# x @ w_in of later items as three float32r products of exactly split factors, with the first sums scaled in PSUM

## Chip, core and metric

The kernel runs on one core of one Trainium2 chip. The metric is device time in microseconds for one launch, inputs and outputs in HBM. The kernel before has a median of 511.81 us over three runs (511.08 to 513.34).

## What is computed

An mLSTM cell is followed by a two-layer block. B = 4, H = 8 heads, S = 768 steps, D = 40; the 3072 tokens have 320 features, w_in is 320 x 2048, w_out 2048 x 320. Everything is float32, w_in and w_out arrive as float64 bits.

```python
for t in range(S):                       # the cell, per batch and head
    m_new = maximum(f[t] + m, i[t])
    f_stab, i_stab = exp(f[t] + m - m_new), exp(i[t] - m_new)
    C = f_stab * C + i_stab * outer(v[t], k[t])
    n = f_stab * n + i_stab * k[t]
    y[t] = sigmoid(o[t]) * (C @ q[t]) / maximum(abs(n @ q[t]), 1)
x = y as (B * S, H * D)                  # 3072 x 320
h = x @ w_in
out = (h - tanh(h)) @ w_out
```

## The kernel before, in words

The cell is worked in 24 units, each 128 tokens of one batch; two units make a token group g (256 tokens, 12 groups). The features of x lie on partitions: `xT[g % 6]` is 128 x 3 x 256, three overlapping blocks of features. The 2048 hidden features are eight pairs p of two 128-wide blocks (i = 0, 1). One step of the block is a group with a pair, (g, p), 96 in all. An **item** is two such steps done together (the first two items have one), 49 items, numbered x = 0 to 48. From item 17 on an item is (g, p) and (g, p + 1) of one group, four items per group: pairs 0 and 1, 2 and 3, 4 and 5, 6 and 7, for g = 4 to 11.

For an item, `up` (line 1084) makes h: per pair and block two full products of 128 features (line 1099, with the weight column chosen by `col`, the x block by `at`) and a rest of 64 features (line 1099 or, in quarters, line 1104). `ph[i]` is a PSUM bank of 128 x 512: two pairs of 256 tokens. There is one such bank per block, so the next item may start on a bank only when it has been read. `shrink` (line 1160) makes g = h - tanh(h): ScalarE squares (`z`, then `q`), VectorE makes `gt` from h and z (the cube) and then from q. `sums_of_g` adds four more VectorE sums (`s`). `down_seven` (line 972) multiplies with w_out by a seven-product scheme, k = 0 to 6, 14 products per item; products 3 to 6 use the sums `s`, products 0, 1 and 2 use gt alone. It runs one item later (LAG = 1): while item x is in `up`, item x - 1 becomes ready for `down_seven`. At the last item of a group, `put_together` reads the result banks on ScalarE and VectorE and stores.

Items 0 to 16 and units 0 to 11 are ordered by a planner (class Plan, line 157): each operation has an engine, an assumed duration, what it comes after and a rank; the planner simulates the engines and takes the operation that can start first, ties by rank, lower first. From item 17 the order is written out in the loop at line 1576: TensorE's steps of one iteration (`dense`) are the item's `up`, its rests with the scores of a new unit (`crossed_scores`), the rest of the unit scored before (`block_turned`), and `down_seven` of item x - 1. Steps of other engines are spread over iterations with `spread_over` at positions x0 to x1 counted in items, and `merge` (line 1207) sets them between TensorE's steps by the share of the assumed cost that is done. Each engine keeps this order (class Pinned, line 96, and T). Units 12 to 23 get a slot of two items each; their x goes through DRAM (`turn_by_store`, line 792): four stores and then two loads into xT, issued on SyncE's queue.

The helper lines 106, 129 and 133 record the instructions of all engines, so profiles are read by tile names. PE names: `ph_up` is x @ w_in, `pS` and `po` are x @ w_out (gt @ w_out), `ps` scores, `pT` and `pc` the rest of a unit, `awake` fill that keeps the clock up. DVE is VectorE, ACT ScalarE, POOL GpSimd, SP SyncE.

Of the kernel before, what the change touches and what calls it, by code (L numbers as in the profile page):

```python
# [50 lines left out]
BF = mybir.dt.bfloat16  # L51
I32 = mybir.dt.int32
# [8 lines left out]
L = 128  # L61
# [14 lines left out]
ROUND = 1.5 * 2.0 ** 23  # L76


@with_exitstack
def kernel(  # L80
# [239 lines left out]
    w_in = const.tile([128, NP, WP], FP, name="w_in")  # L320
# [19 lines left out]
    ld = {}  # L340

# [8 lines left out]
    def load_unit(n, names=("kz", "qz", "v", "k", "o", "q2"), queue=SP, behind=(), crossed=False):  # L350
# [3 lines left out]
        for name in names:  # L354
# [22 lines left out]
            elif c:  # L377
                t["q2"] = load.tile([TOP, len(TRIOS), L], FP, name="q2", tag="q2", bufs=3)
                for i in range(TRIO):
                    queue.dma_start(out=t["q2"][i * D:(i + 1) * D, 0:len(range(i, H, TRIO))], in_=qT[b, c, :, slice(i, H, TRIO)])  # L380
# [7 lines left out]
    diag = const.tile([128, H, L], BF, name="diag")  # L388
# [154 lines left out]
    def weights(dst, srcs, queue):  # L543

        p, n = dst.shape
        w = {}
        src = srcs[0][-1]

        def fetch(behind=()):
            to = dst  # L550
            if src.dtype != FP:
                to = w["st"] = conv.tile([128, n], I64, name="w64", tag="w64", bufs=4)[0:p]
            for rows, cols, part in srcs:
                view = to[rows, cols]
# [30 lines left out]
        def product():  # L585
            V.tensor_tensor(out=dst, in0=w["r"], in1=w["e"].bitcast(FP), op=OP.mult)
# [5 lines left out]
    def blocks_of(p):  # L592
# [9 lines left out]
        for i in range(2):  # L602
            whole.append((slice(i * HALF, (i + 1) * HALF), slices(4, 1), moe_w_in[half[i]:half[i] + HALF, slices(2 * p + i, 1)]))
        return (weights(w_in[:, p, :], whole, G),
                weights(w_out[:, 2 * p:2 * p + 2, :].rearrange("p two n -> p (two n)"),
# [3 lines left out]
    parts_of = [const.tile([L, GT, DM], FP, name=f"part{g}") for g in range(FIRST)]  # L609
# [37 lines left out]
    def scaled(n, i, name, bufs, by_heads=False):  # L647

        t = un[n]
        flat = att.tile([L, H * D1 + HALF - D1], FP, name=name, tag=name, bufs=bufs)  # L650
# [134 lines left out]
    def keep_x(n):  # L785
        g, tt = divmod(n, GT)
        A.copy(out=xT[g % NX][:, :, tt * L:(tt + 1) * L], in_=un[n]["px"])
# [4 lines left out]
    def turn_by_store(n):  # L792
# [12 lines left out]
        for i in range(2):  # L805
            half = slice(i * HALF, (i + 1) * HALF)
            SP.dma_start(out=xT[g % NX][half, :, tt * L:(tt + 1) * L], in_=rows.rearrange("(c p) t -> p c t", p=128)[half])
# [164 lines left out]
    def down_seven(some):  # L972
# [20 lines left out]
        for k in (0, 1, 5, 3, 4, 2, 6) if final else range(7):  # L993
# [89 lines left out]

    def up(some, shrink, quarters=False):
# [4 lines left out]
        def product(i, x, j):  # L1089
# [3 lines left out]
            if j < NK:  # L1093
                col = (i, 3 - i)[j]
                lhs, rhs = w_in[:, p, col * 128:(col + 1) * 128], xT[g % NX][:, at, :]
            else:
                rows = slice(i * HALF, (i + 1) * HALF)
                lhs, rhs = w_in[rows, p, 2 * NK * 128:], xT[g % NX][rows, at, :]
            T.matmul(ph[i][:, x, :], lhs, rhs, start=(x == 0 and j == 0), stop=(j == NK), skip_group_check=True)

        def quarter(i, x, c):
            g, p = some[x]
            rows, cols, first = slice(i * HALF, (i + 1) * HALF), slice(c * HALF, (c + 1) * HALF), 2 * NK * 128 + c * HALF
            T.matmul(ph[i][cols, x, :], w_in[rows, p, first:first + HALF], xT[g % NX][rows, ((0, 2, 1), (0, 1, 2))[i][NK], :],
                     start=False, stop=True, skip_group_check=True)

# [5 lines left out]
        return full, (rest, [lambda: shrink(some, ph)])  # L1112
# [289 lines left out]
    def plan_weights(p, rank, at):  # L1402
        for k, block in enumerate(blocks_of(p)):
# [9 lines left out]
            converted[p, k] = plan.add("V", 0.75, product, [op] + (of_tokens[NT - 1] + of_states[NT - 1] if p >= KEPT else []), r, give=[("w", held)])  # L1413
# [24 lines left out]
    def plan_item(x):  # L1438
# [26 lines left out]
        op = plan.add("T", 0.43 * n, rest, [op], rank, tiles=2, dense=0.7)  # L1465
# [64 lines left out]

    for x in range(START):
        plan_item(x)
    busy = []
# [41 lines left out]
    news = []  # L1575
    for x in range(START, len(items) + LAG):
# [222 lines left out]
```

## Time and profile before

| | |
|---|---|
| timed runs, median (lowest to highest) | 511.81 us (511.08 to 513.34) |
| span of the profiled execution (the only time of it that is shown) | 518.8 us |
| PE busy | 512.1 us, 99% |
| PE weight loads busy | 441.9 us, 85% |
| DVE busy | 371.7 us, 72% |
| ACT busy | 205.6 us, 40% |
| granted TensorE clock, mean | 1.00 |
| x @ w_in on PE, all shapes | 227.0 us in 1344 instructions |

The span runs from the first to the last instruction of one execution under the profiler. A line of a group gives engine, operation, out<-in by tile, shapes and count, then busy time, mean ns of one, idle time of its engine just before, and what ended that idle time. A matmul's mean reaches to the end of its pipeline, so the distance of the starts, not the mean, is its price in a row of matmuls. A line of the timeline gives start, duration, engine, line, operation and count of a merged run.

### The profile page before, as it was taken

How to read it: one execution, taken by the hardware profiler on the slowest of the kernel's cores; microseconds unless marked ns; L12 is line 12 of the kernel's file. 1: busy time of each engine (PE TensorE's matmuls, PEld its weight loads, DVE VectorE, ACT ScalarE, POOL GpSimd, SP SyncE). 2: the span in 40 equal slices, each digit the busy share in tenths (PEclk: the TensorE clock that was granted, in tenths of full speed). 3: DMA queues.
4: the chain of work that ended last, by engine and by line, in shares of the span. 5: the costliest groups of instructions: out<-in, count | busy, mean ns of one | idle time of the engine just before them, and what ended most of it. 6: DMA issues, size and time to landing. Idle time of an engine off the chain costs nothing.

```text
span 518.8 us, 11220 instructions
## 1 busy us (share of the span) xinstructions
PE 512.1 (99%) x4281; PEld 441.9 (85%) x4281; DVE 371.7 (72%) x840; ACT 205.6 (40%) x523; POOL 40.3 (8%) x88
## 2 busy tenths in 40 slices
PE   9999999999999999999999999999999999999996
PEld 5778878888889888898988988988988989888885
DVE  3589969998865766687785785786776767764634
ACT  3167489476564242423323323323324224231412
POOL 4421414330000000000000000000000000000000
PEclk9999999999999999999999999999999999999999
DMA  7968456554000300005344355344334442320001
GB/s 230 270 183 249 118 174 178 169 106 104 9 1 6 92 27 10 18 27 106 69 109 104 73 121 115 73 115 105 70 104 100 76 116 33 69 57 0 27 2 31
DMA packets 112420, 47.26 MB, mean 91 GB/s; under 512 B 87080, under 2 KB 106088, under 8 KB 112360
## 3 DMA queue, kind: packets, MB, share of 16 engines
q1 hardware_dynamic: 106128, 31.72, 27.3%
q0 software_dynamic: 3040, 10.82, 7.0%
q10 hardware_dynamic: 3192, 3.93, 2.2%
q8 instruction: 36, 0.59, 0.5%
q14 instruction: 24, 0.20, 0.1%
HBM read 36.75 MB, written 9.44 MB: 89 GB/s over the span
## 4 chain that ended last, share of the span: by engine, by line
PE 98%; ACT 1%; DVE 0%; issue 0%
PE ph_up L129 41%; PE pS L129 31%; PE po L129 7%; PE ph L129 5%; PE ps L129 4%; PE awake L129 3%; PE pT L129 3%; PE pc L129 2%; PE px L133 1%; ACT vs L106 0%; PE gate L129 0%; ACT L106 0%; PE gate L133 0%; DVE ob L106 0%; ACT part L106 0%; ACT o L106 0%
## 5 line engine op out<-in xcount | busy, mean ns | idle before, releaser
L129 PE MATMUL ph_up<-xT,w_in 128*128 128x256 f32 (+2 forms) x1344 | 227.0, 386 | 0.0
L129 PEld LDWEIGHTS ph_up<-xT,w_in 128*128 128x128 f32 (+2 forms) x1344 | 171.5, 173 | 37.3 <-issue 15.3
L106 ACT ACTIVATE z<-ph_up 128x512 f32<-128x512 f32 (+1 forms) x98 | 56.9, 584 | 242.0 <-PE ph_up L129 122.2
L106 DVE SCALAR_TENSOR_TENSOR gt<-ph_up,z 128x512 f32<-128x512 f32 (+1 forms) x98 | 63.5, 676 | 67.1 <-ACT z L106 66.8
L129 PE MATMUL pS<-wT,s 128*128 128x160 f32 x480 | 72.0, 299 | 0.0
L129 PEld LDWEIGHTS pS<-wT,s 128*128 128x128 f32 x480 | 67.4, 190 | 0.0
L106 ACT ACTIVATE q<-z,tiny 128x512 f32<-128x512 f32 (+1 forms) x98 | 66.3, 711 | 1.0
L106 DVE SCALAR_TENSOR_TENSOR gt<-q,gt 128x512 f32<-128x512 f32 (+1 forms) x98 | 63.3, 678 | 0.0
L129 PE MATMUL pS<-w_out,gt 128*128 128x160 f32 x320 | 54.3, 312 | 0.0
L129 PEld LDWEIGHTS pS<-w_out,gt 128*128 128x128 f32 x320 | 44.6, 189 | 6.5 <-issue 3.6
L106 DVE TENSOR_TENSOR P<-ps,over 128x384 f32<-128x384 f32 x24 | 12.3, 553 | 36.4 <-PE ps L129 36.4
L129 PE MATMUL po<-w_out,gt 128*128 128x320 f32 x128 | 38.2, 441 | 0.0
L106 DVE TENSOR_TENSOR s<-gt 128x256 f32<-128x256 f32 x80 | 30.3, 420 | 0.0
L129 PEld LDWEIGHTS po<-w_out,gt 128*128 128x128 f32 x128 | 23.1, 190 | 8.5 <-issue 0.3
L129 PEld LDWEIGHTS ph<-vs,P 128*128 128x128 f32 x192 | 27.4, 215 | 1.0 <-issue 0.6
L129 PE MATMUL pS<-wT,gt 128*128 128x160 f32 x160 | 28.3, 299 | 0.0
L129 PE MATMUL pS<-w_out,s 128*128 128x160 f32 x160 | 28.3, 299 | 0.0
L129 PEld LDWEIGHTS ps<-qz,kz 40*64 40x64 f32 (+1 forms) x576 | 25.1, 163 | 3.2 <-DVE vs L106 0.8
L129 PE MATMUL ph<-vs,P 128*128 128x41 f32 x192 | 27.5, 294 | 0.0
L129 PE MATMUL ps<-qz,kz 40*128 40x128 f32 (+2 forms) x576 | 26.1, 267 | 0.0
L129 PEld LDWEIGHTS pS<-wT,gt 128*128 128x128 f32 x160 | 23.9, 190 | 0.0
L129 PEld LDWEIGHTS pS<-w_out,s 128*128 128x128 f32 x160 | 23.9, 190 | 0.0
(114 smaller groups left out, 502.4 us busy)
## 6 DMA issues: line engine op xcount, KB each, us to landing
w<-in_moe_w_out POOLq DMA_DIRECT2D x8, 640.0 KB, 6.2
w<-in_moe_w_in POOLq DMA_DIRECT2D x16, 256.0 KB, 5.2
kz<-in_kT SPq DMA_DIRECT2D x48, 80.0 KB
o<-in_o_gate SPq DMA_DIRECT2D x24, 160.0 KB
qz<-in_qT SPq DMA_DIRECT2D x44, 80.0 KB
out<-ob ACTq DMA_DIRECT2D x11, 320.0 KB
h_rows<-zt SPq DMA_DIRECT2D x48, 64.0 KB
z_in<-h_rows SPq DMA_DIRECT2D x48, 64.0 KB
```

The lines of the kernel that those rows point to most:

```text
L106: i = method(*args, **kwargs)
L129: return cls.keep(nc.tensor.matmul(*args, **kwargs))
L133: return cls.keep(nc.tensor.transpose(*args, **kwargs))
```

## The change

float32r is a second way to give float32 data to TensorE. Each weight w of a pair is split into an upper part u and a lower part `low`, w = u + low; each x into 4096 x' + l. The sum w x is then written as

(u x' + low l) * 4097 + (u - 4096 low)(l - x'),

three products in place of the four of a full multiplication. The first two are summed in PSUM, ScalarE multiplies that sum in place by 4097 (`scale`), and the third accumulates on top. The rests of 64 features stay in float32, so each pair keeps its `w_half` and each group its float32 x.

Weights of pairs 0 to 5 are split by `split_in` (two ScalarE and two VectorE steps per pair; u takes the place of the pair's float32 weights); pairs 0 and 1 and the x of group 4 in the planned part (`plan_thirds`), pairs 2 to 5 in items 17 to 20. The parts lie in what earlier stages have left free, so the steps of pair 3 go in four runs of 128 columns and those of pair 5 in three. `split_x` (one ScalarE, two VectorE instructions over 128 x 768) makes a group's parts in the last item of the group before. An item uses the new form if both its pairs and its group's x are split when its iteration begins (`in_thirds`); pairs 6 and 7 never are.

Two of the seven products of an item's `down_seven` (k = 1 and 2) are held back (`tail`) and put into the next iteration, behind the first sums of the new form, or ahead of `up` where it has the old form. Items whose `down_seven` is that of a group's last item, and item 17, hold nothing back.

Beside that, `w_in` becomes a tile per pair plus a half tile per pair, so that the last step of converting w_in from float64 bits is two VectorE instructions; the groups from 6 on share two x tiles (4 + g % 2); `q2` is a fixed tile of three buffers; the first gate rows lie in x tiles.

```diff
+SHIFT = 2.0 ** 12
+CUT = 1.0 - 2.0 ** -13
...
-    w_in = const.tile([128, NP, WP], FP, name="w_in")
+    w_in = [const.tile([128, 2 * NK * 128], FP, name="w_in", tag=f"w_in{p}") for p in range(NP)]
+    w_half = [const.tile([128, 128], FP, name="w_half", tag=f"w_half{p}") for p in range(NP)]
     w_out = const.tile([128, NFF, DM], FP, name="w_out")
-    xT = [const.tile([128, NK + 1, TG], FP, name=f"xT{i}") for i in range(NX)]
+    x_tiles = {}
+    def x_tile(g):
+        if g not in x_tiles:
+            tag = g if g < NX and not general else FIRST + g % 2
+            x_tiles[g] = const.tile([128, NK + 1, TG], FP, name="xT", tag=f"xT{tag}")
+        return x_tiles[g]
+    general = []
...
-    f_sb, i_sb, m_sb, lf = (t.rearrange("p k n -> p (k n)")[0:BH, i * S:(i + 1) * S] for t in (w_out[:, 2 * KEPT:], w_in[:, KEPT:]) for i in range(2))
+    f_sb, i_sb = (w_out[:, 2 * KEPT:].rearrange("p k n -> p (k n)")[0:BH, i * S:(i + 1) * S] for i in range(2))
+    m_sb, lf = (const.tile([128, S], FP, name="rows", tag=f"xT{i}")[0:BH] for i in (FIRST, FIRST + 1))
...
-            V.tensor_tensor(out=dst, in0=w["r"], in1=w["e"].bitcast(FP), op=OP.mult)
+            for x, a, b in places:
+                V.tensor_tensor(out=x, in0=w["r"][:, a:b], in1=w["e"].bitcast(FP)[:, a:b], op=OP.mult)
...
-    def down_seven(some):
+    def down_seven(some, order=range(7)):
...
-        for k in (0, 1, 5, 3, 4, 2, 6) if final else range(7):
+        for k in (0, 1, 5, 3, 4, 2, 6) if final else order:
...
+    w_thirds, x_thirds = {}, {}
+    def in_thirds(some):
+        return all(p in w_thirds for _, p in some) and some[0][0] in x_thirds
...
+    def split_in(p):
+        low, cross = homes(p)
+        runs = []
+        for k in range(4):
+            old = runs[-1] if runs else None
+            if old and all(home[old[0]][0] == home[k][0] and home[k][1] - home[old[0]][1] == k - old[0] for home in (low, cross)):
+                old[1] = k + 1
+            else:
+                runs.append([k, k + 1])
+        w = w_in[p]
+        held = {}
+        def at(home, a, b):
+            return places[home[a][0]][:, home[a][1]:home[a][1] + b - a].rearrange("p k n -> p (k n)")
+        def each(step):
+            for a, b in runs:
+                step(a, b, slice(a * 128, b * 128))
+        def first():
+            each(lambda a, b, cols: A.activation(out=at(cross, a, b), in_=w[:, cols], func=AF.Copy, scale=CUT))
+        def second():
+            each(lambda a, b, cols: V.tensor_tensor(out=at(low, a, b), in0=w[:, cols], in1=at(cross, a, b), op=OP.subtract))
+        def third():
+            held["u"] = const.tile([128, 2 * NK * 128], FR, name="w_high", tag=f"w_in{p}")
+            each(lambda a, b, cols: A.copy(out=held["u"][:, cols], in_=at(cross, a, b)))
+        def fourth():
+            each(lambda a, b, cols: V.scalar_tensor_tensor(out=at(cross, a, b), in0=at(low, a, b), scalar=-SHIFT, in1=at(cross, a, b), op0=OP.mult, op1=OP.add))
+            w_thirds[p] = ([held["u"][:, k * 128:(k + 1) * 128] for k in range(4)], *([places[t][:, k] for t, k in home] for home in (low, cross)))
+        return first, second, third, fourth
+    def split_x(g):
+        x, l, d = (const.tile([128, NK + 1, TG], FR, name="x_thirds", tag=f"xT{k}") for k in range(3))
+        def upper():
+            A.activation(out=x, in_=x_tile(g), func=AF.Copy, scale=CUT / SHIFT)
+        def lower():
+            V.scalar_tensor_tensor(out=l, in0=x, scalar=-SHIFT, in1=x_tile(g), op0=OP.mult, op1=OP.add)
+        def crossed():
+            V.tensor_tensor(out=d, in0=l, in1=x, op=OP.subtract)
+            x_thirds[g] = x, l, d
+        return upper, lower, crossed
...
+        def third(i, x, j, k):
+            g, p = some[x]
+            at, col = ((0, 2), (0, 1))[i][j], (i, 3 - i)[j]
+            T.matmul(ph[i][:, x, :], w_thirds[p][k][col], x_thirds[g][k][:, at, :], start=(x == j == k == 0), stop=False, skip_group_check=True)
+        def scale(i):
+            A.mul(out=ph[i][:, 0:n], in_=ph[i][:, 0:n], mul=SHIFT + 1.0)
         full = [(0.43, lambda i=i, x=x, j=j: product(i, x, j)) for i in range(2) for x in range(n) for j in range(NK)]
         if quarters:
             rest = [lambda i=i, x=x, c=c: quarter(i, x, c) for x in range(n) for c in range(2) for i in range(2)]
         else:
             rest = [lambda i=i, x=x: product(i, x, NK) for x in range(n) for i in range(2)]
-        return full, (rest, [lambda: shrink(some, ph)])
+        last = [lambda: shrink(some, ph)]
+        if not in_thirds(some):
+            return full, (rest, last)
+        sums = [[(0.12, lambda i=i, x=x, j=j, k=k: third(i, x, j, k)) for k in ks for x in range(n) for j in range(NK)]
+                + [(0.0, lambda i=i: scale(i))] * (ks[0] == 0) for ks in ((0, 1), (2,)) for i in range(2)]
+        return sums, (rest, last)
...
-            converted[p, k] = plan.add("V", 0.75, product, [op] + (of_tokens[NT - 1] + of_states[NT - 1] if p >= KEPT else []), r, give=[("w", held)])
+            converted[p, k] = plan.add("V", 0.75, product, [op] + (of_tokens[NT - 1] + of_states[NT - 1] if p >= KEPT and k == 1 else []), r, give=[("w", held)])
...
+    def plan_thirds():
+        steps = []
+        op = plan.add("A", 0.9, lambda: [steps.extend(split_x(FIRST)), steps[0]()],
+                      [units[n]["x"] for n in range(FIRST * GT, (FIRST + 1) * GT)] + [ups[x] for x in range(START - 2)], 50.0)
+        for i in (1, 2):
+            op = plan.add("V", 0.95, lambda i=i: steps[i](), [op], 50.0)
+        op = None
+        for p in range(2):
+            steps_of_p = []
+            for i in range(4):
+                op = plan.add("VA"[i % 2 == 0], 0.7, lambda p=p, i=i, steps=steps_of_p: [steps.extend(() if i else split_in(p)), steps[i]()],
+                              ([op] if op else []) + ([units[n]["second"] for n in range(PLANNED)] if p else [ups[x] for x in range(START) if any(run[1] == 0 for run in items[x])]), 60.0)
+    plan_thirds()
...
+    late = [(p, START + (p - 2) * 0.4, START + (p - 1) * 0.4) for p in (2, 3)] + [(p, START + 1.6 + (p - 4) * 0.8, START + 2.4 + (p - 4) * 0.8) for p in (4, 5)]
+    splits = {p: [] for p, _, _ in late}
+    for p, x0, x1 in late:
+        spread_over([(0.0, lambda p=p, i=i: [splits[p].extend(() if i else split_in(p)), splits[p][i]()]) for i in range(4)], x0, x1)
+    EARLY, LATE_ONES = (0, 3, 4, 5, 6), (1, 2)
+    news, tail = [], []
     for x in range(START, len(items) + LAG):
...
-            dense, rest = up(some, shrink(x), bool(scored or new[:1]))
+            products, rest = up(some, shrink(x), bool(scored or new[:1]))
+            g, p = some[-1]
+            again = []
+            if p == NP - 1 and g + 1 < NG:
+                again = split_x(g + 1)
+            if in_thirds(some):
+                dense += products[0] + products[1]
+                dense += [(0.0, step) for step in again[:2]] + tail + products[2] + products[3]
+            else:
+                dense += tail + products
+                dense += [(0.0, step) for step in again[:2]]
             dense.append((0.6 + 0.9 * len(new[:1]), lambda: halves(rest, *(crossed_scores(n) for n in new[:1]))))
+            dense += [(0.0, step) for step in again[2:]]
             for n in scored:
                 dense.append((1.9, lambda n=n: [block_turned(n), Clock.later("turned", 1.2, lambda: [turn_back(n), n + B < NU and keep_halves(n)])]))
+        else:
+            dense += tail
         dense += [(0.9, lambda n=n: halves(crossed_scores(n))) for n in new[1 if x < len(items) else 0:]]
+        tail = []
         some = tuple(run[:2] for run in items[x - LAG])
-        if in_seven(*some[0]):
+        if x == START or some[-1][1] == NP - 1:
             dense += down_seven(some)
         else:
-            for i, run in enumerate(items[x - LAG]):
-                dense += down(i, some, *run)
+            steps = down_seven(some, (*EARLY, *LATE_ONES))
+            dense, tail = dense + steps[:-2 * len(LATE_ONES)], steps[-2 * len(LATE_ONES):]
```

The function `homes` names the tiles in which the parts of a pair lie: a new tile for pair 0, the `q2` tile for pair 1, `diag` and `part0` for pair 2, corners of `part0`, `part1` and others for pair 3, `part2` and an x tile for pair 4, `part3`, corners and that x tile for pair 5. The code behind the branch at the end, which runs only when a bound is exceeded, is adapted to the new tiles.

More of the change, by code (lines that the diff above doesn't have):

```diff
@@ L51 @@
 BF = mybir.dt.bfloat16
+FR = mybir.dt.float32r
 I32 = mybir.dt.int32
@@ L377, in load_unit @@
             elif c:
-                t["q2"] = load.tile([TOP, len(TRIOS), L], FP, name="q2", tag="q2", bufs=3)
+                t["q2"] = load.tile([TOP, len(TRIOS), L], FP, name="q2", tag="kz", bufs=3) if general else q2[0:TOP, n % 3]
                 for i in range(TRIO):
@@ L384 @@
     load_unit(0, ("kz",))
[L388 removed]
+    diag = const.tile([128, H, L], BF, name="diag", tag="diag")
     V.memset(diag[:, 0], 1.0)
@@ L543, in weights @@
     def weights(dst, srcs, queue):
-        p, n = dst.shape
+        p, n = 128, sum(x.shape[1] for x in dst)
         w = {}
         src = srcs[0][-1]
+        places, at = [], 0
+        for x in dst:
+            places.append((x, at, at + x.shape[1]))
+            at += x.shape[1]
         def fetch(behind=()):
-            to = dst
             if src.dtype != FP:
-                to = w["st"] = conv.tile([128, n], I64, name="w64", tag="w64", bufs=4)[0:p]
+                w["st"] = conv.tile([128, n], I64, name="w64", tag="w64", bufs=4)[0:p]
             for rows, cols, part in srcs:
-                view = to[rows, cols]
+                if src.dtype != FP:
+                    view = w["st"][rows, cols]
+                else:
+                    x, a, b = next(place for place in places if place[1] <= cols.start < place[2])
+                    view = x[rows, cols.start - a:cols.stop - a]
                 if len(part.shape) == 3:
@@ L603, in blocks_of @@
             whole.append((slice(i * HALF, (i + 1) * HALF), slices(4, 1), moe_w_in[half[i]:half[i] + HALF, slices(2 * p + i, 1)]))
-        return (weights(w_in[:, p, :], whole, G),
-                weights(w_out[:, 2 * p:2 * p + 2, :].rearrange("p two n -> p (two n)"),
+        return (weights((w_in[p], w_half[p]), whole, G),
+                weights((w_out[:, 2 * p:2 * p + 2, :].rearrange("p two n -> p (two n)"),),
                         [(every, slice(0, 2 * DM), moe_w_out[slices(2 * p, 2), :].rearrange("(two p) n -> p two n", two=2))], G))
-    parts_of = [const.tile([L, GT, DM], FP, name=f"part{g}") for g in range(FIRST)]
+    parts_of = [const.tile([L, GT, DM], FP, name="part", tag=f"part{g}") for g in range(FIRST)]
     part = [parts_of[n // GT][:, n % GT] for n in range(FIRST * GT)]
@@ L806, in turn_by_store @@
             half = slice(i * HALF, (i + 1) * HALF)
-            SP.dma_start(out=xT[g % NX][half, :, tt * L:(tt + 1) * L], in_=rows.rearrange("(c p) t -> p c t", p=128)[half])
+            SP.dma_start(out=x_tile(g)[half, :, tt * L:(tt + 1) * L], in_=rows.rearrange("(c p) t -> p c t", p=128)[half])
     def in_halves(b):
@@ L1652, in begin_any @@
         row = t["P"].rearrange("p i j t -> p (i j t)")
-        V.tensor_tensor_scan(out=row, data0=row, data1=diag.rearrange("p h t -> p (h t)"), initial=0.0,
+        V.tensor_tensor_scan(out=row, data0=row, data1=general[-1].rearrange("p h t -> p (h t)"), initial=0.0,
                              op0=OP.mult, op1=OP.add)
@@ L1745 @@
                 full, half = up(((g, p0), (g, p0 + 1)), lambda _, phs: gts.extend(shrink_any(ph) for ph in phs))
-                for _, step in full:
+                for _, step in sum(full, []) if in_thirds(((g, p0), (g, p0 + 1))) else full:
                     step()
```

43 lines of the change are left out of this document (32 added, 11 removed).

## Prediction

> **What bounds the kernel now.** I read the first page first: who is busy, and whose chain ended last.
>
> ```profile
> PE 512.1 (99%) x4281; PEld 441.9 (85%) x4281; DVE 371.7 (72%) x840; ACT 205.6 (40%) x523; POOL 40.3 (8%) x88
> ...
> PE 98%; ACT 1%; DVE 0%; issue 0%
> ```
>
> TensorE makes the end: of the chain of waits 98% is its own work, so a microsecond taken off its order of instructions is a microsecond off the span, as long as nothing else makes it wait. The chain in order of time shows what one item of the stage that is changed consists of. Item 25 (pairs 0 and 1 of token group 6) has its x @ w_in before this excerpt; the excerpt holds its scores and then items 26 and 27.
>
> ```profile
> 294.06 0.67 PE ps L129 x32
> 294.73 4.00 PE pS L129 x28
> 298.73 4.48 PE ph_up L129 x32
> 303.20 1.11 PE pT L129 x48
> 304.31 0.60 PE pc L129 x16
> 304.91 4.00 PE pS L129 x28
> 308.91 4.48 PE ph_up L129 x32
> ...
> 318.06 2.16 PE ph_up L129 x10
> ```
>
> There is no gap in it. Of the 4.48 us of ph_up, 16 instructions are the full 128-row products that the change touches; the other 16 are the 64-row rests, which stay. The stretches by engine say how much room the others have (columns: stretch, length, busy time with count for PE, weight load, DVE, ACT and POOL, clock, DMA share, GB/s).
>
> ```profile
> 31.00:213.00 182.00, 181.14 (x1169) 153.39 (x1169) 145.95 (x300) 101.84 (x263) 26.30 (x46) 1.00 0.35 98
> 213.00:508.00 295.00, 295.00 (x2928) 261.88 (x2927) 205.07 (x486) 91.49 (x234) 1.60 (x15) 1.00 0.34 73
> 213.00:251.00 38.00, 38.00 (x431) 33.93 (x430) 30.08 (x75) 11.55 (x29) 0.39 (x4) 1.00 0.23 51
> ```
>
> From 213 us on (items 17 to 48, the written-out order) DVE is busy 205.07 of 295, ACT 91.49. In items 17 to 20 (213 to 251 us) DVE already has 30.08 of 38.
>
> **Removed: fp32 products.** The prices of TensorE come from this stretch of the timeline, where four kinds follow each other without a gap, and from item 27.
>
> ```profile
> 27.86 1.24 PE L129 MATMUL awake<-diag 128*128 128x512 bf16 x5
> 28.94 1.87 PE L129 MATMUL ph<-vs,P 128*128 128x41 f32 x16
> 30.65 0.84 PE L129 MATMUL pc<-vs,k 128*120 128x123 f32 x6
> 31.32 1.07 PE L129 MATMUL ph_up<-xT,w_in 128*128 128x256 f32 x4
> ...
> 308.61 3.35 PEld L129 LDWEIGHTS ph_up<-xT,w_in 128*128 128x128 f32 x16
> 308.75 3.62 PE L129 MATMUL ph_up<-xT,w_in 128*128 128x256 f32 x16
> ...
> L129 PE MATMUL ph_up<-xT,w_in 128*128 128x256 f32 x768 | 176.4, 380 | 0.0
> ```
>
> 384 full products (96 pairs, two blocks, two chunks) show as 768 instructions: one fp32 product is two instructions. Item 27's sixteen take 3.62 us, the last one 0.38 to its end: (3.62 - 0.38) / 15 = 0.216 apart. The bf16 row shows what that is: five instructions of 512 columns start 28.94 - 27.86 = 1.08 us before the next kind, 0.216 each too. An fp32 instruction of 256 columns thus costs what 512 streamed columns cost, and a product of two such instructions streams its 256 columns four times. 16 x 0.216 = 3.46 us per item.
>
> Which items change: a pair counts when its weights and its group's x are already split when the item begins. Pairs 0 and 1 are split before item 17, 2 and 3 during it, 4 and 5 only by item 20; so two items of group 4 and three each of groups 5 to 11, **23 items**.
>
> **Added on TensorE: 24 float32r products per item** (3 products x 2 blocks x 2 chunks x 2 pairs). No float32r instruction is in the trace. Its lower bound is a stream of 256 columns once, half the bf16 row: 0.108 us. The upper bound is an fp32 instruction: 0.216. A second floor is the load of 128 weight columns for each: in the row ph<-vs,P only 2 x 41 columns are streamed, and still 16 instructions take 30.65 - 28.94 = 1.71, 0.107 each; that is the load. Does it hide behind the stream? The pc row has both at once: 2 x 123 columns streamed (0.104 by the bf16 row), loads of 120 columns, and (31.32 - 30.65) / 6 = 0.112 each, not the sum of the two. So I take 0.110, near the lower end, because loads and streams of about that length overlap in these rows: 24 x 0.110 = 2.64. Saved: 3.46 - 2.64 = 0.82 per item, 23 x 0.82 = **18.9 us**. At the upper end it would be 24 x 0.216 = 5.18, a loss of 1.72 per item.
>
> The Trainium skill has a rule that speaks against this (TensorE: Matmul & The Clock Gate, Part 3, The mechanism): weight loads are said to overlap matmuls in flight only when the row group differs. By that rule each float32r product would cost load plus stream and the item would be slower; the pc row, with all 128 rows in both, contradicts it. The same skill (FP8 and Floating Point Precision, TensorE Precision Notes) says that reduced-precision fp32 reads four bytes and truncates, and true fp32 needs four passes; by it float32r is one pass, which no run here shows yet.
>
> **Added on ACT, and the new wait.** Two scalings per item, 128x512 in PSUM. Nearest rows, PSUM to SBUF and SBUF to SBUF:
>
> ```profile
> L106 ACT ACTIVATE q<-z,tiny 128x512 f32<-128x512 f32 x64 | 42.6, 718 | 0.0
> L106 ACT ACTIVATE z<-ph_up 128x512 f32<-128x512 f32 x64 | 37.7, 594 | 195.9 <-issue 113.2 <-PE ph_up L129 76.1 <-PE pc L129 6.6
> ...
> 298.56 4.64 PE L129 MATMUL ph_up<-xT,w_in 128*128 128x256 f32 x32
> 303.31 0.60 ACT L106 ACTIVATE z<-ph_up 128x512 f32<-128x512 f32 x1 [4.80 <-PE ph_up L129]
> 303.81 0.20 ACT L106 ACTIVATION_READ_ACCUMULATOR z<-ph_up 128x1 f32 x1
> 304.04 1.29 DVE L106 SCALAR_TENSOR_TENSOR gt<-ph_up,z 128x512 f32<-128x512 f32 x2 [0.58 <-ACT z L106]
> ```
>
> I take 0.60 (bounds 0.53, a little under z, to 0.72). 2 x 23 of them, 28 us, lie in 196 us of idle time of ACT ahead of z; what matters is the wait. The third product of a block accumulates on the scaled sum, so TensorE's next load waits for ACT, and everything behind it (rests, scores, x @ w_out: the whole chain) waits too. Lags: z starts at 303.31, 0.11 after the products end at 298.56 + 4.64 = 303.20; a product starts 308.75 - 308.61 = 0.14 after its load; gt starts 0.03 after ACT's end (303.81 + 0.20); with 0.06 for that signal I take 0.20 from ACT's end to the product. Counting from an item's first product: block 0's eight start by 0.77 and end 0.27 later (0.11 stream and 0.38 - 0.216 = 0.16 pipe); scaling 0 runs 1.15 to 1.75, product resumes at 1.95 where 16 x 0.11 = 1.76 was free: 0.19 lost. Block 1's last starts at 1.65, scaling 1 runs 2.03 to 2.63, resume 2.83; the four of block 0 are done at 1.95 + 0.44 = 2.39: 0.44 lost. **0.63 us per uncovered item.**
>
> The change covers it with x @ w_out work held back from the item before last: two of seven products, 8 instructions. From the chain, 4.00 / 28 = 0.143 each, 1.14 us; then block 0 goes on at 1.76 + 1.14 = 2.90 > 1.95, block 1 at 3.34 > 2.83, nothing lost and 0.5 us to spare. But no work is held back by items whose x @ w_out ends a group, nor at the start: so item 17 and every item of pairs 2 and 3 (groups 4 to 11) have no cover. 9 x 0.63 = **+5.7 us** (0.53 or 0.72 for a scaling, and a signal of 0 or 0.11, give 0.50 and 0.80: 4.5 to 7.2). Holding back is itself free: the same instructions, moved. It brings the next item's first product 1.14 us closer to the last rests: 4.00 - 1.14 = 2.86 us behind them. DVE must by then have read block 0; z 0.60, then the cube of 0.69 below, is about 1.5 us after the rests. Late next there would be the second cube at 2.1.
>
> **Added on DVE and ACT: the splits.**
>
> ```profile
> L106 DVE SCALAR_TENSOR_TENSOR gt<-ph_up,z 128x512 f32<-128x512 f32 x64 | 41.2, 686 | 43.8 <-ACT z L106 43.8
> L106 DVE SCALAR_TENSOR_TENSOR gt<-q,gt 128x512 f32<-128x512 f32 x62 | 40.4, 677 | 0.0
> L106 DVE TENSOR_TENSOR s<-gt 128x256 f32<-128x256 f32 x62 | 23.4, 420 | 0.0
> ...
> L106 DVE TENSOR_TENSOR wT<-w_out 128x160 f32<-128x160 f32 x8 | 2.5, 318 | 0.0
> ...
> 310.02 1.27 SPq L106 DMA_DIRECT2D xT<-y_rows  x2
> ```
>
> From 0.420 at 256 columns and 0.677 at 512, one column costs 1.0 ns: 768 columns 0.93. x of a group: two on DVE, 1.9 us, one on ACT (about 1.0), in the last item of the group before. In steady state DVE then has 1.9 us more per four items of about 36, of which it works some 25: hidden. ACT's split waits for x: xT<-y_rows is issued at 310.02 in item 27; the split for that group follows the products of item 28, which begin at 318.06. Even two saved 0.82s leave some 8 us, so ACT and the squares queued behind it don't wait. SP's stores go to two x buffers instead of six, but each comes after the last read of the group two before: no wait.
>
> Weights: two DVE and two ACT instructions per pair of 0.68 and 0.72, but for pair 3 in four runs and pair 5 in three (some 0.25 each, by the 128x160 row). Pairs 2 to 5 fall into items 17 to 20: on DVE 2 x 1.36 + 8 x 0.25 + 6 x 0.3 = 6.5 us, and 1.9 for group 5's x: 8.4 us more. 30.08 + 8.4 = 38.5 us of work in a stretch of under 38: **there DVE runs over**, and as its order is fixed the cubes that free PSUM come late. If later slack takes it all, 0; if all lies on the path, +8.4. I take **+3.0**, a little over the excess. Pairs 0 and 1 and group 4's x (4.6 us on DVE), and the conversion of w_in in two instructions instead of one (8 x 0.2), fall into the planned stage, DVE 146 of 182 us. The planner's order moves with them; I take **+0.5** (bounds -2 and +4).
>
> **The sum.** -18.9 + 5.7 + 3.0 + 0.5 = -9.7 us. The profiled execution has a span of 518.8; nothing else of its own time is shown, and the median of the three timed runs, 511.81, lies 7 us below it. I carry the difference over as it is: 509.1 in a profile, 511.8 - 9.7 = **502 us** timed.
>
> **Rivals.** (1) The waits vanish: scalings start earlier than modelled and DVE's excess is absorbed. -18.9 + 9 x 0.2 = -17: 495 us. For it: 44 us in which DVE waits for z could be used; against it: its order is fixed. Chance 0.08. (2) DVE becomes the bound where the splits are: 8.4 of the splits and 4 of the planned stage on the path, -18.9 + 5.7 + 12.4 = -0.8: 511 us. For it the 30.08 of 38; against it that the chain has 0% of DVE now. Chance 0.18, half of it over the line to faster. (3) The other side: **float32r costs as much as an fp32 instruction**, since it is streamed twice, or since its load doesn't hide (0.107 + 0.108 = 0.215). 24 x 0.216 = 5.18 per item, 23 x 1.72 = +39.6; scalings are then better covered (9 x 0.2 = 1.8), with 3.5 for the splits: +45, 557 us. It decides from a spacing of 0.130 us on: there 23 x (3.46 - 24 x 0.130) = 7.8 no longer pays for 5.7 + 3.5. For it: no such instruction in the trace; against it the pc and bf16 rows. Chance 0.05 for the stream and 0.04 for the load. The overlap rule of the Trainium skill named above (TensorE: Matmul & The Clock Gate, Part 3, The mechanism) is the second of these. (4) The condition on split weights and x fails when the program is written out, and fp32 products stay: 512 us, 0.03.
>
> **How the numbers follow.** Forecast 0.62, its own range 498 to 507, most of what the bounds of its three costs allow. The range for 8 in 10 takes in most of rival 2 and some of rival 1: 495 to 510. About 0.5% (2.6 us) is what a measurement of this kernel tells from no change. Faster: 0.62 + 0.08 + 0.09 = 0.79; same: half of rival 2 and most of rival 4, 0.11; slower: 0.10.
>
> **What would show it.** Groups by shape: 552 float32r matmuls of 128x256 at about 0.110 apart, 400 fp32 ones left (768 - 23 x 16). In the chain, ACT ph_up appears ahead of x @ w_in in items of pairs 2 and 3 with some 0.6 us each, and not in others. In items 17 to 20 DVE is near full, and TensorE waits for gt. Wrong would be: spacing over 0.130, scalings on the chain in covered items, or a planned stage that ends over 2 us earlier or 4 later than 213.

## The result and the profile after

The changed kernel takes 507.71 us (median of five runs, 506.40 to 520.00) against 511.81 of the kernel before on the same chip; the ratio is 0.990, with a 95% interval of 0.987 to 0.993. So it is faster by about 1%, some 5 us, and by about half of the 9.7 us that were forecast. The time lies inside the range.

One of the five runs of each kernel took 520 us or more and is left out of the ratio, and both profiled executions, before (518.8 us of span) and after (517.9), had a start in which TensorE ran at half rate until about 27 and 31 us, so below they are compared stretch by stretch from the first items on and not by their spans.

The page after, its busy times, its chain of waits and four of its groups:

```profile
PE 505.5 (98%) x4465; PEld 444.7 (86%) x4465; DVE 393.0 (76%) x886; ACT 245.5 (47%) x599; POOL 39.9 (8%) x88
...
PE 83%; DVE 11%; ACT 3%; issue 2%; DVEq 0%; ACTq 0%
...
L138 PE MATMUL ph_up<-xT,w_in 128*128 128x256 f32 x400 | 93.4, 382 | 0.6 <-DVE gt L115 0.6
...
L138 PE MATMUL ph_up<-x_thirds,w_thirds 128*128 128x256 f32 x368 | 57.6, 289 | 4.2 <-ACT ph_up L115 4.2
...
L115 ACT ACTIVATE ph_up<-ph_up 128x512 f32<-128x512 f32 x46 | 26.8, 582 | 48.7 <-PE ph_up L138 38.5
...
L138 PE MATMUL ph_up<-x_thirds,w_high 128*128 128x256 f32 x184 | 31.5, 293 | 0.0
```

The change was made as described: 368 + 184 = 552 float32r products and 400 fp32 instructions are left, 23 items with two scalings each (46). But TensorE no longer has the chain to itself: it went from 98% to 83%, and VectorE has 11% and ScalarE 3%. These shares say where the chain was followed, not what each engine cost (the part on the steady stretch shows why). The idle time in front of the products now has a releaser, ACT ph_up, with 4.2 us.

Where it changed is read by cutting the span at the last rest of items 16, 20, 44 and 48. The stretches by engine (columns as in the prediction: stretch, length, then busy time with count for PE, weight load, DVE, ACT and POOL, clock, DMA share, GB/s), first of the kernel before, then after:

```profile
207.90:244.80 36.90, 36.90 (x368) 32.67 (x368) 28.53 (x69) 11.81 (x30) 0.18 (x2) 1.00 0.19 44
244.80:471.50 226.70, 226.70 (x2374) 202.03 (x2368) 160.97 (x384) 70.66 (x181) 1.42 (x13) 1.00 0.41 87
471.50:505.60 34.10, 34.10 (x210) 29.80 (x209) 17.67 (x36) 10.25 (x25) 0.00 (x0) 1.00 0.03 10
```

```profile
209.90:252.60 42.70, 39.40 (x384) 35.03 (x386) 32.96 (x84) 20.05 (x53) 0.18 (x2) 0.92 0.16 37
252.60:470.90 218.30, 217.09 (x2518) 201.28 (x2512) 173.06 (x402) 96.09 (x223) 1.42 (x13) 1.00 0.42 91
470.90:503.50 32.60, 32.40 (x234) 29.60 (x232) 17.67 (x36) 13.73 (x31) 0.00 (x0) 1.00 0.03 11
```

| stretch | before | after | difference | forecast |
|---|---|---|---|---|
| planned part (item 0's rests to item 16's) | 172.8 | 172.9 | +0.1 | +0.5 |
| items 17 to 20 | 36.9 | 42.7 | +5.8 | +2.6 |
| items 21 to 48 | 260.8 | 250.9 | -9.9 | -12.8 |
| sum | | | -4.0 | -9.7 |

The forecast column only sorts the prediction's terms by where they lie: two changed items without cover and the +3.0 are in items 17 to 20 (2 x (-0.82 + 0.63) + 3.0), the other 21 items, seven of them without cover, behind it. The trace's -4.0 agrees with the timed runs (-4.1 between the medians, -5.2 by the ratio) to about a microsecond, for two parts of the span lie outside the table: the start up to item 0's rests is 2.0 longer after, and what follows item 48's last rest is 1.1 longer (14.0 against 12.9; 12.8 to 13.7 in the other runs of whole kernels). Only 0.2 of that 1.1 is TensorE's; why the rest behind its last product differs from run to run stays open. So there are two things to explain: the steady part gained 2.9 less, and the four items in which the weights are split lost 3.2 more.

**The steady part.** The chain after, in order of time, for item 23 (pairs 0 and 1) and, behind the dots, for the scaling of item 26, which has no cover:

```profile
276.19 1.89 PE ph_up L138 x16
278.08 1.09 PE pS L138 x8
279.17 1.97 PE ph_up L138 x24
281.14 0.67 PE ps L138 x32
...
306.05 0.41 DVE ob L115
306.46 0.57 ACT ph_up L115
...
307.08 1.76 PE ph_up L138 x20
```

Sixteen float32r products take 1.89 us: 0.118 each, not 0.110. The eight held back products (pS, 1.09) stand between the first sums and the last eight products, and no ACT stands there: a covered item, one whose scalings have such products beside them, waits for nothing. By 3.46 - 24 x 0.118 it saves 0.63 us, and the covered items measure just that (10.18 to 9.55 between last rests, in other slots 8.52 to 7.89). Item 26 has ACT ph_up in the chain; such items save only 0.14 and 0.17 (9.15 to 9.01 and 8.52 to 8.35), so the wait takes 0.46 to 0.49. DVE ob ahead of it isn't what it waited for: by the trace's releasing event `ob` ends at 306.464 us, and the scaling had begun at 306.447. The last product of block 1's first sums ended at 306.411, 0.036 earlier, and all 46 scalings but the late one of item 17 begin 0.036 or 0.037 us behind their products. So the chain went over to VectorE here because a neighbour ended at the same moment, and the VectorE steps before it are not on the path.

**Items 17 to 20.** Where the 42.7 us go shows in the kernel after in four views. First the stretches by engine, of 5 us each:

```profile
213.00:218.00 5.00, 3.66 (x30) 3.46 (x28) 4.83 (x13) 1.68 (x5) 0.00 (x0) 1.00 0.00 0
218.00:223.00 5.00, 3.80 (x44) 2.86 (x48) 0.71 (x2) 1.65 (x4) 0.00 (x0) 0.57 0.02 3
223.00:228.00 5.00, 5.00 (x41) 4.88 (x35) 4.21 (x16) 3.63 (x14) 0.00 (x0) 0.74 0.00 0
```

Then ScalarE's timeline (start, duration, engine, operation, count, idle time before and its releaser):

```profile
215.29 0.58 ACT L115 ACTIVATE ph_up<-ph_up 128x512 f32<-128x512 f32 x1 [1.19 <-PE ph_up L138]
218.05 0.62 ACT L115 CAST w_high<-w_thirds 128x512 fp32r<-128x512 f32 x1 [2.17 <-DVE w_thirds L115]
218.57 0.58 ACT L115 ACTIVATE ph_up<-ph_up 128x512 f32<-128x512 f32 x1
```

TensorE's timeline, with the same columns:

```profile
219.20 1.22 PE L138 MATMUL ph_up<-x_thirds,w_thirds 128*128 128x256 f32 x4 [2.54 <-ACT ph_up L115]
220.35 1.99 PE L138 MATMUL ph_up<-xT,w_half 64*64 64x256 f32 x16
222.12 1.50 PE L138 MATMUL ps<-qz,kz 40*64 40x128 f32 x32
...
231.80 1.09 PE L138 MATMUL ph_up<-xT,w_half 64*64 64x256 f32 x16
...
248.31 3.69 PE L138 MATMUL ph_up<-xT,w_in 128*128 128x256 f32 x16 [0.56 <-DVE gt L115]
```

And the chain of waits in order of time (start, duration, what):

```profile
213.60 0.68 DVE gt L115
214.28 0.68 DVE s L115 x2
...
216.93 0.49 DVE vs L115
217.41 0.61 DVE w_thirds L115
218.03 0.02 issue
218.05 0.62 ACT w_high L115
218.66 0.49 ACT ph_up L115
```

In item 17 ScalarE does scaling 0 at 215.29, then in its fixed order the copy of pair 2's upper part (w_high), and only then scaling 1. The copy needs VectorE's subtraction (w_thirds), which is queued behind the cubes, the sums s, the sums of wT and a unit's vs: VectorE works 4.83 of 5 us there. So ScalarE stands (is idle) for 2.17 us, scaling 1 comes at 218.57, and TensorE stands for 2.54 us. Behind the stand its clock is down to 0.57 and then 0.74: the same sixteen rests take 1.99 us where they take 1.09 one item later, and scores and x @ w_out are stretched too. Item 17 takes 11.77 us and item 18 10.81 where they measured 8.31 and, in its fp32 form, 9.15 when nothing stood in the way (the run with the splits spread out, below).

### The profile page after: what moved, and what is told of

It is laid out like the page before. It is cut to its first block, busy times and chain, and to the rows that moved or that the text cites. A ratio compares the mean times of both kernels' runs of the same rounds, so it can differ in the third digit from the quotient of the medians.

```text
span 517.9 us, 11777 instructions
## 1 busy us (share of the span) xinstructions
PE 505.5 (98%) x4465; PEld 444.7 (86%) x4465; DVE 393.0 (76%) x886; ACT 245.5 (47%) x599; POOL 39.9 (8%) x88
## 4 chain that ended last, share of the span: by engine, by line
PE 83%; DVE 11%; ACT 3%; issue 2%; DVEq 0%; ACTq 0%
PE ph_up L138 34%; PE pS L138 22%; PE po L138 7%; PE ph L138 6%; PE ps L138 4%; PE awake L138 3%; DVE gt L115 3%; DVE s L115 3%; PE pT L138 2%; PE pc L138 2%; DVE ob L115 1%; PE px L142 1%; DVE P L115 1%; ACT ph_up L115 1%; DVE wT L115 1%
## 5 line engine op out<-in xcount | busy, mean ns | idle before, releaser
L138 PE MATMUL ph_up<-xT,w_in 128*128 128x256 f32 x400 | 93.4, 382 | 0.6 <-DVE gt L115 0.6
L138 PEld LDWEIGHTS ph_up<-xT,w_in 128*128 128x128 f32 x400 | 74.0, 190 | 10.3 <-issue 0.8
L138 PE MATMUL ph_up<-x_thirds,w_thirds 128*128 128x256 f32 x368 | 57.6, 289 | 4.2 <-ACT ph_up L115 4.2
L138 PE MATMUL pS<-w_out,gt 128*128 128x160 f32 x320 | 58.9, 315 | 0.0
L138 PE MATMUL ph_up<-xT,w_half 64*64 64x256 f32 (+1 forms) x576 | 54.7, 401 | 0.0
L138 PEld LDWEIGHTS ph_up<-x_thirds,w_thirds 128*128 128x128 f32 x368 | 48.9, 190 | 6.0 <-ACT ph_up L115 6.0
L138 PEld LDWEIGHTS pS<-w_out,gt 128*128 128x128 f32 x320 | 46.5, 193 | 6.2 <-issue 3.6
L115 ACT ACTIVATE ph_up<-ph_up 128x512 f32<-128x512 f32 x46 | 26.8, 582 | 48.7 <-PE ph_up L138 38.5
L138 PEld LDWEIGHTS ph_up<-xT,w_half 64*64 64x64 f32 (+1 forms) x576 | 29.0, 152 | 15.2 <-issue 8.2
L138 PE MATMUL ph_up<-x_thirds,w_high 128*128 128x256 f32 x184 | 31.5, 293 | 0.0
```

Source lines behind the costliest of these rows:

```text
L115: i = method(*args, **kwargs)
L138: return cls.keep(nc.tensor.matmul(*args, **kwargs))
```

## The experiments

Each ratio below is to the kernel before, timed beside that run.

**What a float32r product costs.** A program with nothing but rows of 32 products each on TensorE, one kind after another; it computes none of the kernel.

```python
def stream(name, kind, cols, n, count):     # kind: fp32, float32r or bf16 operands
    bank = ps.tile([128, 512], FP, name=name, tag="bank" + str(len(name) % 2))
    t = w[kind]
    for i in range(count):
        k = i % 4
        m = nc.tensor.matmul(bank[0:cols, 0:n], t[:, k * 128:k * 128 + cols], t[:, 512:512 + n], start=True, stop=True)
        ...
```

> No part of the computation, only streams of 32 matmuls of one shape each, with a new weight block every time; the result is zeros. Theory A (a float32r instruction is bound by its weight load of about 0.118 us): 128 columns of weights with 512 streamed are 0.216 apart, 64 columns with 256 are 0.109. Theory B (it streams once, with some 0.010 us of its own on top): 128 x 512 at 0.226, 64 x 256 at 0.118. Forecast's value: 128 x 256 at 0.110; the trace of the changed kernel says 0.118.

Groups of that program (r: float32r, h: bf16, f: fp32; then the weight columns; 128x n is the result; busy us, mean ns):

```profile
L35 PE MATMUL r64by<-round 128*64 128x512 f32 x32 | 7.6, 394 | 0.1
L35 PE MATMUL r128by<-round 128*128 128x512 f32 x32 | 7.6, 393 | 0.1
L35 PE MATMUL f128by<-plain 128*128 128x64 f32 x64 | 7.4, 276 | 0.1
L35 PE MATMUL r128by<-round 128*128 128x384 f32 x32 | 5.7, 334 | 0.0
L35 PE MATMUL r128by<-round 128*128 128x256 f32 x32 | 4.2, 288 | 0.0
L35 PE MATMUL r64by<-round 128*64 128x256 f32 x32 | 3.8, 276 | 0.0
L35 PE MATMUL h128by<-half 128*128 128x256 bf16 x32 | 3.7, 272 | 0.1
```

(Busy minus one mean, over the count less one, is the mean distance of the starts in a row: (3.7 - 0.272) / 31 = 0.11 for bf16. For float32r with 128 columns by 256 it is 0.126, because the first distance, from the start of the row, is 0.305; so medians follow.) The starts themselves have median distances of 0.109 for bf16 at 256 columns, 0.113 for float32r with 64 weight columns, 0.120 with 128 (0.116 the shortest); 0.173 at 384 columns; at 512, 0.227 with 128 weight columns and 0.230 with 64. One fp32 instruction of 256 columns takes 0.216, and of 64 columns 0.112; a quarter of the columns would stream in 0.054, so there it is most likely the weight load that counts. So float32r streams once and its load is hidden, but its stream is some 5% slower per column than bf16 (0.227 against the 0.216 that bf16 takes for 512 in the profile before), and with a load of 128 columns to be hidden behind only 256 columns a few ns more are lost. It is not the load that sets 0.118: with half the load 0.113 remains, and at 512 columns, where the load has twice the room, the stream alone is 0.227. So theory A is out (0.227, not 0.216), and of theory B the single stream holds but not the fixed 0.010 us per instruction: 0.113 and 0.227 are in proportion to the columns.

**The scalings left out.** The two steps `scale(i)` are not issued; h is then not x @ w_in.

```diff
-                + [(0.0, lambda i=i: scale(i))] * (ks[0] == 0) for ks in ((0, 1), (2,)) for i in range(2)]
+                for ks in ((0, 1), (2,)) for i in range(2)]
```

> The two scalings per item are left out, so h of these items is not x @ w_in. It shows what all waits for them cost. Theory: 9 uncovered items x 0.45 plus item 17's 2.5 us of standing and some of the half clock behind it, 5 to 8 us faster than the changed kernel. Rival (scalings are hidden, the loss is VectorE's work): under 3 us. If covered items paid as well, over 10 us.

Measured: 501.06 us (500.22 to 503.27, ratio 0.978, 0.974 to 0.982). Covered items take 9.55 as with scalings, uncovered ones 8.54 instead of 9.01: the scaling costs nothing where it is covered and 0.47 where it isn't. Items 17 to 20 take 38.2 instead of 42.7. Of these 4.5 us, 0.9 are the ordinary waits of items 17 and 18 (2 x 0.47), so 3.6 of the loss need the scalings. The rest doesn't: in TensorE's timeline the end of that stretch still waits for VectorE.

```profile
232.53 3.69 PE L138 MATMUL ph_up<-xT,w_in 128*128 128x256 f32 x16 [1.44 <-DVE gt L115]
```

With no scaling to be late, VectorE is late with the cubes that item 20 needs: the wait that the prediction named, at 1.44 us.

**Cover for the items of pairs 2 and 3.** The last item of a group also holds back products 1 and 2, and `put_together` moves behind them.

```diff
-        if x == START or some[-1][1] == NP - 1:
+        if x == START or x == len(items):
...
-            dense, tail = dense + steps[:-2 * len(LATE_ONES)], steps[-2 * len(LATE_ONES):]
+            kept = 2 * len(LATE_ONES) + (some[-1][1] == NP - 1)
+            dense, tail = dense + steps[:-kept], steps[-kept:]
```

> The last item of a group holds back two of its seven products too, so that the items of pairs 2 and 3 have work to cover the scalings (item 17 still has none). Theory (uncovered scalings cost 0.45 us each): 8 x 0.45 = 3.6 us faster than the changed kernel, and ACT ph_up goes from the chain in those items. Rival: the result of a group comes 1.1 us later, its banks come free later, and the next group's x @ w_out waits for VectorE instead: within 1 us of the changed kernel.

Measured: 507.37 us (504.76 to 517.14, ratio 0.987, 0.983 to 0.991). The seven items concerned drop from 9.01 to 8.54 and from 8.35 to 7.88, as without scalings. The timed runs can't tell this from the change as it was (0.990, 0.987 to 0.993); in the trace, of the 7 x 0.47 = 3.3 us, 2.2 arrive in items 21 to 48 (248.7 against 250.9): item 43 took 8.66 instead of 7.90, and items 37 and 39 0.1 to 0.2 more. The waits around item 43 (engine and tile, what it waited for: us in total, times, longest) have

```profile
DVE den L115 <- DMA z_in<-h_rows: 1.1, 1, 1.1
PEld pS L138 <- DVE ob L115: 1.1, 2, 0.8
```

A unit's `den` on VectorE waits for a transfer, the sums of the result (ob), now later in VectorE's order, stand behind it, and the next x @ w_out finds its banks unread. The same edit in the last run below did not show it (7.90), so how often it happens stays open.

**Nothing held back at all.**

```diff
-        if x == START or some[-1][1] == NP - 1:
+        if True:
```

> No item holds back products, so every float32r item stands uncovered before its third products. Theory: an uncovered scaling costs 0.47 us, a covered one nothing: 14 more items pay, 6.6 us slower than the changed kernel. Rival (x @ w_out behind the rests hides nothing or the wait is longer without it): no change, or over 10 us.

Measured: 513.34 us (512.19 to 516.24, ratio 1.002, 0.999 to 1.005). The fourteen covered items take 0.46 to 0.48 more (10.02 instead of 9.55), 6.4 us in items 21 to 48 against 1.2 less in items 17 to 20 (41.5), and that takes back what the change gained: without the held back products the change makes no difference that can be measured.

**The order on ScalarE.** To tell whether the loss in item 17 is due to the place of the copy between the scalings or to VectorE's excess, the splits of pairs 2 and 3 begin at 0.45 of item 17 instead of 0, behind both scalings, and still end within it.

```diff
-    late = [(p, START + (p - 2) * 0.4, START + (p - 1) * 0.4) for p in (2, 3)] + [...]
+    late = [(p, START + 0.45 + (p - 2) * 0.27, START + 0.45 + (p - 1) * 0.27) for p in (2, 3)] + [...]
```

> Only the place of the splits of pairs 2 and 3 is changed: they begin at 0.45 of item 17 (behind its rests) and end within it, so the same items use float32r. Theory (ScalarE's queue): in the changed kernel the copy of pair 2's upper part waits for VectorE between the two scalings of item 17, so TensorE stands 2.5 us and then works some 2.5 us at half clock; both go, 3 to 5 us faster than the changed kernel, and no idle time of PE behind ACT ph_up over 0.6 us is left. Rival (VectorE's excess of work in items 17 to 20): the same work is still there, the time stays within 1 us of the changed kernel and TensorE waits somewhere else in items 17 to 20.

Measured: 507.55 us (505.56 to 516.49, ratio 0.988, 0.985 to 0.991): no difference from the change as it was that the timed runs can tell. TensorE's timeline:

```profile
216.38 0.74 PE L138 MATMUL ph_up<-x_thirds,w_thirds 128*128 128x256 f32 x4 [0.20 <-ACT ph_up L115]
...
225.15 1.18 PE L138 MATMUL ph_up<-x_thirds,w_high 128*128 128x256 f32 x2 [1.94 <-ACT w_high L115]
```

Item 17 is cured (8.31 instead of 11.77), but item 18 rises from 10.81 to 13.05: it needs pair 3's parts, which now come late, TensorE stands 1.94 us for them, and its clock is 0.71 in the 5 us around. Over items 17 to 20 the trace has 40.7 us instead of 42.7, so moving the copy out from between the scalings gave at most 2.0 of the 5.8 us by which these items are longer than before. Neither reading was right alone: VectorE works 4.86 of the 5 us around that stand too (223 to 228 us), and ScalarE's order mostly decides which of TensorE's steps pays for it.

**The splits spread out.** The same splits take four items instead of two and a half: pairs 2 and 3 from 1.5 to 3.1 items behind the start, pairs 4 and 5 from 3.9 to 5.9. Item 18 then keeps its fp32 products, since pairs 2 and 3 aren't ready.

```diff
-    late = [(p, START + (p - 2) * 0.4, START + (p - 1) * 0.4) for p in (2, 3)] + [(p, START + 1.6 + (p - 4) * 0.8, START + 2.4 + (p - 4) * 0.8) for p in (4, 5)]
+    late = [(2, START + 1.5, START + 2.3), (3, START + 2.3, START + 3.1), (4, START + 3.9, START + 4.9), (5, START + 4.9, START + 5.9)]
```

> The splits of pairs 2 to 5 are spread over items 18 to 22 instead of 17 to 20; item 18 then stays with fp32 products, every other item is as in the changed kernel. Theory (the splits crowd VectorE's and ScalarE's fixed order in items 17 to 20): from the last rest of item 16 to that of item 20 the changed kernel takes 42.7 us against 37.0 before; here it is 37 to 37.5, and the kernel is 5 us faster than the changed one in its trace, 3 to 5 us by time. Rival (the half clock after item 17 or the new place of the buffers is the cause): these four items still take over 40 us and the time stays.

Measured: 503.20 us (502.00 to 512.74, ratio 0.982, 0.978 to 0.985). Items 17 to 20, cut as before:

```profile
199.60:236.40 36.80, 36.60 (x380) 32.74 (x380) 30.87 (x78) 16.47 (x43) 0.18 (x2) 1.00 0.19 43
```

Items 17 to 20 take 36.8 instead of 42.7, with a clock of 1.00, although one item less has the new form; items 21 to 44 take 218.2, what they took. VectorE is busy for 30.87 us of it against 32.96, and for a larger share of the time than before, yet TensorE is idle for 0.2 us only instead of 3.3: what counts is not how full VectorE is, but whether a scaling or a product stands behind the crowd. So the 5.9 us are shown to come from where the splits were put, pressed into too short a stretch, and not from the places of the new buffers, which are the same here.

**Both: spread and covered.**

```diff
+    late = [(2, START + 1.5, START + 2.3), (3, START + 2.3, START + 3.1), (4, START + 3.9, START + 4.9), (5, START + 4.9, START + 5.9)]
...
+        if x == START or x == len(items):
...
+            kept = 2 * len(LATE_ONES) + (some[-1][1] == NP - 1)
```

> Both edits: splits spread over items 18 to 22, and products held back from the last item of each group as well. Theory: the two gains add up, 5 us in items 17 to 20 and 7 x 0.47 less about 1 in items 21 to 47, 7 us less than the changed kernel in the trace, about 501 us. Rival (TensorE's waits for other reasons take their place): not faster than the spread alone.

Measured: 499.40 us (498.89 to 499.98), ratio 0.975, 0.972 to 0.978: it is faster than the kernel before by 2.5%, and than the change as it was. Its stretches by engine, cut at the same items, and then three rows of its chain, of item 22 (pairs 2 and 3), which now has products between and no ACT:

```profile
199.00:235.80 36.80, 36.60 (x378) 32.70 (x378) 30.79 (x79) 16.47 (x43) 0.18 (x2) 1.00 0.19 44
235.80:451.30 215.50, 215.50 (x2520) 200.88 (x2512) 174.81 (x408) 98.65 (x231) 1.42 (x13) 1.00 0.43 92
451.30:483.50 32.20, 32.20 (x236) 29.58 (x232) 17.76 (x36) 13.71 (x31) 0.00 (x0) 1.00 0.04 12
```

```profile
249.37 1.90 PE ph_up L138 x16
251.27 1.09 PE pS L138 x8
252.36 1.97 PE ph_up L138 x24
```

The two edits add up: items 17 to 48 take 36.8 + 215.5 + 32.2 = 284.5 us against 293.6: the 9.1 are, but for rounding, the 5.9 of the one and the 7 x 0.47 = 3.3 of the other. Between 235.80 and 483.50 TensorE has no idle time left.

## Why the prediction was half right

**The sign and the mechanism held.** TensorE's order of instructions set the time, float32r is streamed once with its load hidden, 23 items changed, the scalings are covered where work is held back and bare in the items of pairs 2 and 3, the store and load of x stayed hidden, and the splits made TensorE wait. Three terms of the sum were mis-sized, and in one of them the place was wrong. Two of the errors made the change slower than forecast (23 x 0.19 = 4.4 us by the price, 3.1 by the splits) and two faster (1.5 by the waits, 0.4 by the planned stage), so a part of them cancelled; with the first two alone the time would have come to 509.6, at the edge of the range. That much of the number was luck.

**The price of a product** was taken as 0.110, between a load (0.107) and half a bf16 row (0.108). It measured 0.118: float32r is not as fast per column as bf16. The saving per item is 0.63, not 0.82, and of the 18.9 us 23 x 0.63 = 14.5 are left. It was the largest error of the steady part: 21 x 0.19 = 4.0 us there. The bounds (0.108 to 0.216) held, and the point of 0.130 from which the change no longer pays was not reached. The pc row could not show it, for it is fp32, and fp32 streams at bf16's pace: 0.216 for an instruction of 256 columns streamed twice, as for 512 columns of bf16.

**The wait** was taken as 0.63 per uncovered item and measured 0.47 without scalings and with cover alike: 9 x 0.47 = 4.2 instead of 5.7. ScalarE's price was met (0.582 against 0.60); what was off is the way back: from the end of the scaling to the product the chain of item 26 has 0.05 us (306.46 + 0.57 to 307.08), not 0.20; and the products, being slower, cover scaling 0 entirely. This gave 7 x 0.16 = 1.1 us back in the steady part: -4.0 + 1.1 is the 2.9 by which it fell short.

**The splits** were taken as +3.0 in items 17 to 20 by counting VectorE's work against the stretch. The price of the weight splits was right (6.4 us of them against 6.5; the x of group 5 comes only behind item 20's last rest), and so was the wait for gt in item 20, at 0.56 us. But VectorE did not run over as a whole: it was busy for 32.96 of the 42.7 us, and full only in places (4.83 of 5 us in item 17). What failed is the step from work to wait: an excess over the whole stretch was put behind the cubes, but what paid first was scaling 1 of item 17, queued on ScalarE behind a copy that waits for VectorE. The prediction named the queues behind the transfers and the split of x, and not the one behind the copies of w. By the measured prices items 17 and 18 save 2 x 0.16, so the 5.8 us lost there are 6.1 of the splits: 3.5 in item 17 (11.77 - 8.31; mostly the stand of 2.54, the rest at a lower clock), 1.8 in item 18 (10.81 - 9.01, at the lower clock), 0.8 in item 20 (9.94 - 9.15, with the wait of 0.56). It is inside the bounds of 0 to 8.4; rival 2, the bound on VectorE at 511, gave it all 8.4 with 4 more from the planned stage, which didn't happen.

**The planned stage** was taken as +0.5 and moved by 0.1. The new sum is -14.5 + 4.2 + 6.1 + 0.1 = -4.1; the table of the stretches has -4.0.

The Trainium skill's rule that weight loads overlap matmuls in flight only when the row group differs (TensorE: Matmul & The Clock Gate, Part 3, The mechanism) would give load plus stream, about 0.22 as an estimate (0.107 + 0.113), for these products; the trace has 0.118, so for them it doesn't hold. The four passes that the Trainium skill states for true fp32 (FP8 and Floating Point Precision, TensorE Precision Notes) agree with the trace: a whole fp32 product takes 2 x 0.216, four times the 0.109 of bf16. That float32r is one pass, and a slower one than bf16's, is what the measured 0.113 to 0.118 shows.

## What to carry to other kernels

When work is added to an engine off the path, don't only add it up against the stretch: go through every engine's fixed order and ask which small step of another engine stands behind it, and who waits for that; here a 0.6 us copy on ScalarE, late between two scalings, held TensorE up for 2.5 us. Spread one-time preparation over more of the program than it seems to need, even if an item keeps its old form for it: that was worth 5.9 us in the trace, more than the change had gained. A wait in the middle of a dense order can be covered by independent work from the step before, here at no cost that shows (9.55 us with and without scalings); without it this change gained nothing. And where a chain of waits turns to another engine, compare the times: a releaser that ends when the released step has already begun is none.

## What was not expected of the hardware

**float32r's stream.** 0.227 us for 512 columns against 0.216 of bf16, and 0.118 to 0.120 for 256 with a load of 128 weight columns each.

**The clock behind a short stand.** After TensorE's stand of 2.54 us the granted clock was 0.57 over 5 us, and the instructions behind took up to 1.8 times their time (1.99 us instead of 1.09). The trace's records of the clock have half rate from 218.7 to 225.6 us, so it began while TensorE still stood; in the run with cover, behind the same stand of 2.54, it lasted 3.5 us. It doesn't follow each time: in the run with nothing held back the same stand in item 17 (2.55 us) was followed by rests at the usual pace and a clock of 1.00, as its stretch for items 17 to 20 shows,

```profile
198.60:240.10 41.50, 36.75 (x386) 32.84 (x386) 33.17 (x85) 20.04 (x53) 0.18 (x2) 1.00 0.18 41
```

and yet items 17 to 20 took 41.5 us there, as TensorE then stood for 1.79 in item 20, waiting for VectorE's cubes. By this comparison the slow clock adds only about a microsecond to the whole, and what decides whether it comes wasn't found.

**A start at half rate that the printed clock doesn't show.** TensorE's timeline at the start, first of the kernel after and then of the kernel with both edits:

```profile
9.40 2.34 PE L138 MATMUL awake<-diag 128*128 128x512 bf16 x5
```

```profile
7.44 1.24 PE L138 MATMUL awake<-diag 128*128 128x512 bf16 x5
```

The same five fill products take 2.34 us and 1.24, and the granted clock of both stretches is printed as 1.00. The traces' records of the clock explain this: the first entry, of full rate, stands at 31.0 us in the kernel after, at 27.4 in the kernel before and at 4.0 in the kernel with both edits, and what lies ahead of it is printed as 1.00 because nothing is recorded there. The pace of the fill changes at that entry in each: its starts are 0.43 us apart before it (with both edits too, from 1.5 to 3.2 us) and 0.22 behind it. So that 1.00 is no measurement. All three have the slow start, the kernel before for 27 us, so it isn't the change's; why it lasts so differently stays open.
